# Scanning two tiles at a time, small products on VectorE, and a prologue in another order

## The chip, the cores and the metric

The kernel runs on one core of a Trainium2 chip. The metric is device time in microseconds (us) of one execution. "The span" is the time between the first and the last instruction that the profile shows; the device time of the same execution is a little longer.

## The reference

Three parts follow each other. A linear recurrence (a "state space" scan, here ssm) over 4 batches x 8 heads x 768 positions turns x into y. A dense layer with a gate follows, and then a mixture of eight experts with one expert per token. The core of it:

```python
L = np.exp(cum[:, :, :, None] - cum[:, :, None, :]) * causal
M = np.einsum('bhin,bhjn->bhij', Cc, Bc) * L
y_intra = np.einsum('bhij,bhjd->bhid', M, xc)
y_inter = np.einsum('bhin,bhnd->bhid', Cc, state) * np.exp(cum)[:, :, :, None]
y[:, :, sl] = y_intra + y_inter
state = decay_full[:, :, None, None] * state + np.sum(Bx, axis=2)
...
h = x @ w_in
x = (h * (1.0 / (1.0 + np.exp(-1.702 * h)))) @ w_out
...
expert_idx = np.argmax(logits, axis=1)
out[mask] = gate_w[mask, None] * (np.maximum(x[mask] @ w1[e], 0.0) @ w2[e])
```

There are 3072 tokens, 256 features, 2048 hidden columns in the dense layer, and 8 experts with 1024 hidden columns.

## The kernel before

**Tiles and groups.** The 3072 tokens are 24 tiles of 128 positions; three tiles are a group, so there are groups 0 to 7. A tile holds two chunks of 64 positions, and six tiles are one batch, at whose start the state is empty. The dense layer cuts its 2048 hidden columns into 16 slices f. A **block** (g, f) is `gemm1` (six matmuls of 384 columns, `ph`), `gate` (two ScalarE activations), `low_part` (one VectorE subtraction, `glb`) and `gemm2` (nine matmuls of 256 columns into `po`). Every product runs as three matmuls, on high parts and low parts of both operands, hence yh and yl, and two tiles of each weight (`dw0`, `dw1`).

**The scan of a tile.** `A` scales x (`xtb`). `U` is `ssm_c` (matmuls `pU`) and `ssm_b` (matmuls `pS`). `T` is `ssm_state` (the recurrence on VectorE, `T`), `ssm_pads` (`S`, the state masked for two heads, on GpSimd) and `ssm_mask` (`mt`, on VectorE). `Y` is `ssm_d` (matmuls `pY`, which read mt, xtb and S). `E` is `ssm_e` (`ye` = pY times `ee`, VectorE), `ssm_h` (yh, a cast on ScalarE) and `ssm_l` (yl, a subtraction on GpSimd). pS and pY share one PSUM buffer. `ee` is an exponential per position; for group 0 it is computed on the core (`edge`, `edge_exp`), for the others all rows are computed once (`edge_scale`, matmuls into `ph` and an activation `et`), written to DRAM (`ebuf`) and read back broadcast (`load_ee`).

**The order.** Every engine executes in the order in which the code emits. The string `START` is the prologue, one letter and a number for each step: X and x are edge and edge_exp, N and W load a tile's or a slice's data, A U S T s M Y E H L are the scan's parts, R B u p v h l decode the 16 weight slices from 64-bit words into high and low parts, G g c O are gemm1, gate, low_part and gemm2 of the n-th block, F fills slots in DRAM, r are parts of the router (r4 is edge_scale), i is load_ee, z a route0. The prologue runs the 32 blocks of groups 0 and 1, in turns, and the scans of tiles 0 to 8. A "'" behind a step moves it to its other engine.

After it come six passes `pi` = 1 to 6 of 16 blocks each, for group 2, 3, ..., 7. Within pass pi the tiles of group pi+2 are scanned, each in four steps at a block offset: U and T at k, Y at k+2, E at k+3, with k = 2, 6, 10 (2, 6, 11 in pass 1). The router of the group before (route0 to route4) runs in the same pass. Two blocks are always pending between gemm1 and gemm2, so the last two gemm2 of a group run in the next pass, route0 then copies po (three copies: tile 2 and 0 on VectorE, tile 1 on ScalarE), and the next group's first gemm2 writes the same PSUM. The experts follow behind the passes.

All DMAs but the scatters are issued from SP's queue, in the order of the code, and a DMA whose data or buffer isn't ready holds what is behind it.

Of the kernel before, what the change touches and what calls it, by code (L numbers as in the profile page):

```python
# [10 lines left out]
F32 = mybir.dt.float32  # L11
# [124 lines left out]
def body(ctx, tc, ssm, aall, cst, tok, wcat, emb, tau, w1, w2, out):  # L136
# [39 lines left out]
    sp = early.enter_context(tc.tile_pool(name="sp", bufs=2))  # L176
    late = ExitStack()
# [22 lines left out]
    def load_ee(g):  # L200
        ee = sp.tile([P, TPG, 2, P], F32, tag="ee", name=f"ee{g}")
# [51 lines left out]
    def edge(g):  # L253

        pee = psy.tile([P, 2, 512], F32, tag="sy", name=f"pee{g}")
        cols = al[:, :NTILE * NH].rearrange("p (g q t) -> p g q t", g=NG, q=4)[:, g]
        for j in range(2 * TPG):
            w, o = divmod(j * P, TPG * P)
            for q in range(4):
                nc.tensor.matmul(pee[32 * q:32 * q + 32, w, o:o + P], lhsT=cols[:, q, j:j + 1].to_broadcast([P, 32]),  # L260
                                 rhs=tri, start=(o == 0), stop=True, skip_group_check=True)
        ee_s[g] = pee

    def edge_exp(g):
        pee = ee_s[g]
        ee = sp.tile([P, TPG, 2, P], F32, tag="ee", name=f"ee{g}")
        nc.scalar.activation(out=ee.rearrange("p t k c -> p (t k c)").rearrange("p (w c) -> p w c", w=2),
                             in_=pee[:, :, :TPG * P], func=AF.Exp)
        ee_s[g] = ee
# [55 lines left out]
    def decode_mask(f):  # L325
        v = sp.tile([P, 512], F32, tag="v", name=f"v{f}")
# [14 lines left out]
    Ts = {}  # L341

    def ssm_a(t, eng=nc.gpsimd):
        b, tt = divmod(t, TPB)
        xt = xtb[t % NXT]
        e0 = (b * NCH + 2 * tt) * NPAIR
        eng.tensor_tensor(
            out=xt.rearrange("p c q d -> p (c q) d"), in0=raw_s[t][:, SB2 + SBT:SB2 + SBT + SX].rearrange("p (c d) -> p c d", d=HD),
            in1=einv[:, e0:e0 + 2 * NPAIR].unsqueeze(2).to_broadcast([P, 2 * NPAIR, HD]), op=ALU.mult)
        st.setdefault(t, {})["xt"] = xt  # L350

    def ssm_b(t):

        r = raw_s[t]
        ps = (pre if t < NPRE else psy).tile([P, 2, 512], F32, tag="sy", name=f"pS{t}")
        for c in range(2):
            for w in range(2):
                h = slice(64 * w, 64 * w + 64)
                nc.tensor.matmul(ps[:, w, c * P:(c + 1) * P].rearrange("p (k i) -> p k i", k=2),  # L359
                                 lhsT=r[h, c * P:(c + 1) * P], rhs=cpad(t)[h, :, c, :],  # L360
                                 start=(c == 0), stop=True, skip_group_check=True)
        st.setdefault(t, {})["ps"] = ps

    def ssm_mask(t):
        ps = st[t]["ps"]
        mt = sp.tile([P, 2, 2, 2, Q], F32, tag="mt", name=f"mt{t}")
        nc.vector.tensor_tensor(out=mt.rearrange("p w c k i -> p w (c k) i"),
                                in0=ps[:, :, :256].rearrange("p w (c i) -> p w c i", i=Q),
                                in1=kc[:, K_MASK:K_MASK + Q].unsqueeze(1).unsqueeze(1).to_broadcast([P, 2, 4, Q]),
                                op=ALU.mult)  # L370
        st[t]["mt"] = mt

    def ssm_c(t):
        r, xt = raw_s[t], st[t]["xt"]
        pu = pss.tile([P, 512], F32, tag="m", name=f"pU{t}")
        for c in range(2):
# [4 lines left out]
        st[t]["pu"] = pu  # L381

    def ssm_state(t):

        b, tt = divmod(t, TPB)
        pu = st[t]["pu"]
        e0 = b * NCH + 2 * tt
# [19 lines left out]
    def ssm_pads(t, eng=nc.gpsimd):

        b, tt = divmod(t, TPB)
        c0 = 1 if tt == 0 else 0  # L410
        e0 = b * NCH + 2 * tt + c0 - 1
        n = 2 - c0
        S = sp.tile([P, 2, 2, HD], F32, tag="S", name=f"S{t}")
        eng.tensor_tensor(out=S[:, c0:], in0=Ts[t][:, c0:, :].unsqueeze(2).to_broadcast([P, n, 2, HD]),
                          in1=decm[:, e0:e0 + n, :].unsqueeze(3).to_broadcast([P, n, 2, HD]), op=ALU.mult)
        st[t]["sps"] = [None if c < c0 else S[:, c] for c in range(2)]
        del Ts[t]

    def ssm_d(t):
        xt, mt, sps = st[t]["xt"], st[t]["mt"], st[t]["sps"]  # L420
        py = psy.tile([P, 2, 512], F32, tag="sy", name=f"pY{t}")
# [6 lines left out]
        for c in range(2):  # L428
# [11 lines left out]
        st[t]["py"] = py  # L440

    def ssm_e(t):
        g, tl = divmod(t, TPG)
        py = st[t]["py"]
        if tl == 0:
            yh[g] = yp.tile([P, 2, GT], F32R, tag="yh", name=f"yh{g}")
            yl[g] = yp.tile([P, 2, GT], F32R, tag="yl", name=f"yl{g}")
        ye = sp.tile([P, 2, P], F32, tag="ye", name=f"ye{t}")
        nc.vector.tensor_tensor(out=ye, in0=py[:, :, :P], in1=ee_s[g][:, tl], op=ALU.mult)
        st[t]["ye"] = ye  # L450

    def ssm_h(t, eng=None):
        g, o = t // TPG, t % TPG * P
        (eng.tensor_copy if eng else nc.scalar.copy)(out=yh[g][:, :, o:o + P], in_=st[t]["ye"])  # L454

    def ssm_l(t, eng=nc.gpsimd):
        g, o = t // TPG, t % TPG * P
        ye = st[t]["ye"]
        eng.tensor_tensor(out=yl[g][:, :, o:o + P], in0=ye, in1=yh[g][:, :, o:o + P].bitcast(F32), op=ALU.subtract)  # L459
        del st[t], raw_s[t]  # L460
# [721 lines left out]
```

## Time and profile before

| | |
|---|---|
| three runs | 543.3, 544.15, 544.98 us (median 544.15) |
| the profiled execution | 543.77 us, its span 542.0 us |
| TensorE (PE) busy | 511.6 us of the span |
| VectorE (DVE), ScalarE (ACT), GpSimd (POOL) busy | 335.4, 245.9, 135.0 us |
| one block on PE, nothing between | 2.11 us (1.05 gemm1, 1.06 gemm2) |
| pass 2, from one first gemm2 to the next | 160.30 to 201.08 us |

PE is the engine to watch: where it has no pause, only fewer or cheaper instructions on it help; where it pauses, the question is what it waits for. In a timeline each row is a start, a duration, an engine, a line of the code, an operation, its tiles and a count; a bracket at its end is the time that the engine sat idle before it and what ended that. fp32 matmuls of the scan show two records for each instruction.

### The profile page before, as it was taken

What the parts mean: (1) busy time and instruction counts of PE and PEld (TensorE: products, weight loads), DVE (VectorE), ACT (ScalarE), POOL (GpSimd) and SP (SyncE); (2) the same over time, 40 slices, a digit from 0 to 9 for tenths busy, and PEclk for the clock granted to TensorE, in tenths of its full rate; (3) what the DMA queues carried; (4) which work ended last, traced back from release to release, by engine and by line L of the source; (5) the groups of instructions that cost most, each with busy time, mean ns of one, the idle gap of its engine ahead of it and who ended that gap; (6) DMA issues with size and microseconds to landing.
All of it is one profiled execution on the core that took longest, in us unless ns stands there. A gap on an engine that the chain in (4) does not pass through costs nothing.

```text
span 542.0 us, 13468 instructions
## 1 busy us (share of the span) xinstructions
PE 511.6 (94%) x5392; PEld 485.6 (90%) x5392; DVE 335.4 (62%) x969; ACT 245.9 (45%) x573; POOL 135.0 (25%) x168
## 2 busy tenths in 40 slices
PE   5779999999999999999999999999999999999991
PEld 4569999889989999999999999989999999999991
DVE  3658777766757667657667655866767666555330
ACT  4638666334344344344344344852645435444220
POOL 3433443201431042042042020412311030232022
PEclk9979999989999999999999999999999999999996
DMA  8886874211221121120000005370466442511000
GB/s 304 232 261 183 310 198 143 80 70 40 69 100 40 41 99 40 42 98 2 1 30 2 2 32 195 108 234 20 166 211 207 128 149 96 161 40 49 10 28 28
DMA packets 29052, 57.59 MB, mean 106 GB/s; under 512 B 2790, under 2 KB 19004, under 8 KB 28860
## 3 DMA queue, kind: packets, MB, share of 16 engines
q1 hardware_dynamic: 26492, 50.39, 28.8%
q0 software_dynamic: 2496, 6.32, 3.1%
q8 instruction: 43, 0.70, 0.5%
q14 instruction: 21, 0.17, 0.1%
HBM read 46.05 MB, written 11.01 MB: 105 GB/s over the span
## 4 chain that ended last, share of the span: by engine, by line
PE 70%; issue 13%; DMA 6%; POOL 3%; ACT 2%; DVE 2%; SPq 0%; POOLq 0%; ACTq 0%; DVEq 0%
PE ph L516 21%; PE po L541 17%; PE ph L741 9%; PE qo L767 9%; PE po_a L541 5%; PE pS L359 2%; DMA ee<-ebuf 2%; POOL out L141 2%; DMA wraw<-in_wcat 2%; PE pY L431 2%; PE pY L438 1%; PE pU L379 1%; PE pX L727 1%; DMA slots<-xr,si 1%; DMA wer<-in_w 1%
## 5 line engine op out<-in xcount | busy, mean ns | idle before, releaser
L516 PE MATMUL ph<-yh,dw 128*128 128x384 f32 x512 | 157.2, 347 | 2.5 <-DVE yh L454 1.5
L525 ACT ACTIVATE ghb<-ph 128x384 fp32r<-128x384 f32 x128 | 62.8, 490 | 124.7 <-PE ph L516 124.4
L533 DVE TENSOR_TENSOR glb<-ph,ghb 128x384 fp32r<-128x384 f32 x128 | 70.9, 554 | 74.6 <-ACT ph L526 74.4
L541 PE MATMUL po<-dw,ghb 128*128 128x256 f32 x576 | 107.2, 282 | 1.6 <-ACT xr L554 1.6
L516 PEld LDWEIGHTS ph<-yh,dw 128*128 128x128 f32 x512 | 95.1, 189 | 7.5 <-DVE yh L454 1.6
L541 PEld LDWEIGHTS po<-dw,ghb 128*128 128x128 f32 x576 | 93.1, 188 | 3.3 <-ACT xr L554 3.3
L516 PE MATMUL ph<-yl,dw 128*128 128x384 f32 x256 | 86.6, 338 | 0.5 <-POOL yl L459 0.4
L541 PE MATMUL po<-dw,glb 128*128 128x256 f32 x288 | 81.0, 281 | 0.0
L748 DVE SCALAR_TENSOR_TENSOR glb<-ph,ghb 128x256 fp32r<-128x256 f32 (+5 forms) x72 | 36.6, 508 | 46.3 <-ACT ghb L747 46.1
L747 ACT ACTIVATE ghb<-ph 128x256 fp32r<-128x256 f32 (+5 forms) x72 | 32.6, 453 | 65.7 <-PE ph L741 65.7
L526 ACT ACTIVATE ph<-ph 128x384 f32<-128x384 f32 x128 | 62.2, 486 | 0.0
L141 POOL DMA_INDIRECT out<-ob,xs x29 | 29.8, 1029 | 123.3 <-DVE ob L778 117.3
L767 PE MATMUL qo<-weh,ghb 128*128 128x256 f32 x208 | 58.7, 282 | 0.0
L767 PE MATMUL qo<-wel,ghb 128*128 128x256 f32 x208 | 58.5, 281 | 0.0
L767 PE MATMUL qo<-weh,glb 128*128 128x256 f32 x208 | 58.5, 281 | 0.0
L541 PEld LDWEIGHTS po<-dw,glb 128*128 128x128 f32 x288 | 54.5, 189 | 0.0
L741 PE MATMUL ph<-xh,weh 128*128 128x256 f32 (+5 forms) x160 | 52.7, 329 | 0.6 <-ACT xh L728 0.2
L741 PE MATMUL ph<-xl,weh 128*128 128x256 f32 (+5 forms) x160 | 51.5, 322 | 0.5 <-DVE xl L729 0.4
L741 PE MATMUL ph<-xh,wel 128*128 128x256 f32 (+5 forms) x160 | 51.2, 320 | 0.0
L516 PEld LDWEIGHTS ph<-yl,dw 128*128 128x128 f32 x256 | 48.6, 190 | 1.1 <-POOL yl L459 0.6
L595 DVE SCALAR_TENSOR_TENSOR pr<-xr,enb 128x256 f32<-128x256 f32 x120 | 48.0, 434 | 0.5
L693 DVE TENSOR_TENSOR wel<-wer,weh 128x512 fp32r<-128x512 f32 x60 | 44.7, 749 | 4.4 <-ACT weh L692 3.4
(188 smaller groups left out, 884.7 us busy)
## 6 DMA issues: line engine op xcount, KB each, us to landing
wer<-in_w SPq DMA_DIRECT2D x32, 512.0 KB, 4.1
raw<-in_ssm SPq DMA_DIRECT2D x24, 512.0 KB, 5.3
wraw<-in_wcat SPq DMA_DIRECT2D x16, 512.0 KB, 9.8
slots<-padr SPq DMA_DIRECT2D x8, 516.0 KB, 7.2
ee<-ebuf SPq DMA_DIRECT2D x7, 384.0 KB
xs<-slots SPq DMA_DIRECT2D x3, 516.0 KB, 4.1
xs<-slots SPq DMA_DIRECT2D x3, 387.0 KB
xs<-slots SPq DMA_DIRECT2D x4, 258.0 KB
```

Source lines behind the costliest of these rows:

```text
L141: i = nc.gpsimd.indirect_dma_start(in_offset=None, oob_is_err=False, **kw)
L516: nc.tensor.matmul(ph, lhsT=wslice(w, f, k * P, k * P + P), rhs=y[g][:, k, :], start=(n == 0), stop=(n == 5))
L525: nc.scalar.activation(out=a[:, :GT], in_=ph, func=AF.Gelu_apprx_sigmoid)
L526: nc.scalar.activation(out=ph, in_=ph, func=AF.Gelu_apprx_sigmoid)
L533: nc.vector.tensor_tensor(out=c[:, :GT], in0=ph, in1=a[:, :GT].bitcast(F32), op=ALU.subtract)
L541: nc.tensor.matmul(po[g][tl], lhsT=l, rhs=r, start=(f == 0 and i == 0 and (off + tl) % 2 == 0), stop=(f == NF - 1 and i == 2), skip_group_ ...
L595: nc.vector.scalar_tensor_tensor(out=pr, in0=xr[:, tl, :D], scalar=1.0, in1=enb[:, e, :], op0=ALU.mult, op1=ALU.mult, accum_out=ld[:, tl, ...
L693: eng.tensor_tensor(out=lo[:, o], in0=r, in1=hi[:, o].bitcast(F32), op=ALU.subtract)
L741: nc.tensor.matmul(ph[:, :n], lhsT=w[:, o:o + P], rhs=x[u][:, k, :n], start=(i == 0), stop=(i == 5))
L747: nc.scalar.activation(out=a[:, :n], in_=ph[:, :n], func=AF.Relu)
L748: nc.vector.scalar_tensor_tensor(out=c[:, :n], in0=ph[:, :n], scalar=0.0, in1=a[:, :n].bitcast(F32), op0=ALU.max, op1=ALU.subtract)
L767: nc.tensor.matmul(qacc(u, s), lhsT=l, rhs=r, start=(f == 0 and i == 0 and (s % 2 == 0 or ss is not None)), stop=(f == NFE - 1 and i == 2) ...
```

## The change

It does five things.

1. `START` is written anew. Group 1's ee is computed on the core (X1, x1) and no longer read back (i1 is gone); edge_scale (r4) stands earlier; the fills F stand later; tile 6, 7 and 8 stand apart, over some ten blocks, where they stood close to the end.
2. From tile 10 on, the scan takes a **unit**: a pair (t, 2), or the single tile 9. `ahead` lists the units of each pass. The matmuls are as many as before; the VectorE and ScalarE instructions on a pair take twice the columns, but for `ssm_state`, which stays at one for each chunk.
3. In the passes `ssm_pads` and `ssm_l` run on VectorE.
4. `gemm2` of the first slice of groups 2 to 7 takes its three tiles from the last to the first.
5. Decode buffers have a pool of their own, which is closed before the passes and leaves room for the pairs; ee has three buffers.

```diff
 START = (
-    "X0 W0 x0 u0 N0 N1 S0 B0 W1 A0' U0 N2 W2 M0 S1 R0 T0 N3 p0 R1 A1 u1 U1 T1 s0' Y0 r4 M1 A2 E0 p1 U2 T2 s1 v0 "
+    "W0 u0 B0 X0 x0 R0 N0 S0 A0 M0 U0 N1 W1 B1 N2 R1 N3 T0 s0 p0 v0 r4 W2 u1 N4 h0 S1 A1 U1 T1 M1 A2 Y0 E0 U2 T2 "
...
     def edge(g):
 
-        pee = psy.tile([P, 2, 512], F32, tag="sy", name=f"pee{g}")
+        if g == 0:
+            pee = psy.tile([P, 2, 512], F32, tag="sy", name="pee0")
+            pee = [pee[:, w, :] for w in range(2)]
+        else:
+            pee = [hbank() for _ in range(2)]
...
+    def ssm_c(u):
+        t0, n = unit(u)
+        xt = st[t0]["xt"]
+        pu = pss.tile([P, 512], F32, tag="m", name=f"pU{t0}")
+        for c in range(2 * n):
+            r = raw_s[t0 + c // 2]
             for p in range(NPAIR):
-                o = SB2 + (c * NPAIR + p) * 32
+                o = SB2 + (c % 2 * NPAIR + p) * 32
                 nc.tensor.matmul(pu[32 * p:32 * p + 32, c * HD:(c + 1) * HD], lhsT=r[:, o:o + 32],
                                  rhs=xt[:, c, p, :], start=True, stop=True)
...
     def step(t, what):
         for fn in {"A": (ssm_a,), "U": (ssm_c, ssm_b), "T": (ssm_state, ssm_pads, ssm_mask), "Y": (ssm_d,),
                    "E": (ssm_e, ssm_h, ssm_l)}[what]:
-            fn(t)
+            if fn in (ssm_pads, ssm_l):
+                fn(t, nc.vector)
+            else:
+                fn(t)
...
-        for tl in range(TPG):
+        for tl in (range(TPG) if f or g < 2 else reversed(range(TPG))):
...
-    def tile_steps(jobs, t0, at):
-        for i, k in enumerate(at):
+    def unit_steps(jobs, us, at):
+        for u, k in zip(us, at):
             for d, w in ((0, "U"), (0, "T"), (2, "Y"), (3, "E")):
-                jobs.append((k + d, lambda t=t0 + i, w=w: step(t, w)))
...
+    ahead = {1: [9, (10, 2)], 2: [(12, 2), (14, 2)], 3: [(16, 2)], 4: [(18, 2), (20, 2)], 5: [(22, 2)]}
...
-        if gn < NG:
-            tile_steps(jobs, TPG * gn, (2, 6, 11) if pi == 1 else (2, 6, 10))
...
+        if pi in ahead:
+            unit_steps(jobs, ahead[pi], (3, 10) if pi == 1 else (2, 8))
```

**TensorE in the prologue.** The rows from group 0's ee on (pee0); the number behind a tile's name is the tile of 128 positions, the one behind "_" is a buffer's. ph_287 and ph_247 are edge_scale. Before:

```order
L260 MATMUL pee0_167<-kc_102,al_103 32x128 x24
L359 MATMUL pS0_203<-raw0_199 128x128 x4
L379 MATMUL pU0_213<-xtb0_109,raw0_199 32x32 x8
L359 MATMUL pS1_228<-raw1_201 128x128 x4
L379 MATMUL pU1_248<-xtb1_110,raw1_201 32x32 x8
L431 MATMUL pY0_262<-mt0_226,xtb0_109 32x64 x16
L438 MATMUL pY0_262<-raw0_199,S0_260 32x64 x8
L275 MATMUL ph_287<-kc_102,al_103 96x128 x2
```

With the change (ph_376 and ph_377 are group 1's ee):

```order
L266 MATMUL pee0_177<-kc_105,al_106 32x128 x24
L374 MATMUL pS0_209<-raw0_207 128x128 x4
L398 MATMUL pU0_217<-xtb0_112,raw0_207 32x32 x8
L282 MATMUL ph_247<-kc_105,al_106 96x128 x2
L374 MATMUL pS1_261<-raw1_226 128x128 x4
L398 MATMUL pU1_267<-xtb1_113,raw1_226 32x32 x8
L450 MATMUL pY0_282<-mt0_215,xtb0_112 32x64 x16
L457 MATMUL pY0_282<-raw0_207,S0_242 32x64 x8
L398 MATMUL pU2_311<-xtb2_114,raw2_232 32x32 x8
L374 MATMUL pS2_327<-raw2_232 128x128 x4
L266 MATMUL ph_376<-kc_105,al_106 32x128 x12
L266 MATMUL ph_377<-kc_105,al_106 32x128 x12
```

edge_scale moved from behind tile 0's pY to behind tile 0's pU, and 24 matmuls for group 1's ee are new; between pS2 and them stand tile 1's two pY rows, not shown here.

**SP's queue at the start.** wraw is a slice of weights (W), raw a tile's data (N). Before:

```order
L219 DMA wraw2_224<-in_wcat 128x512
L209 DMA raw3_239<-in_ssm 128x1024
L278 DMA ebuf_82<-et_290 96x2x128
L219 DMA wraw3_422<-in_wcat 128x512
L209 DMA raw4_427<-in_ssm 128x1024
L219 DMA wraw6_459<-in_wcat 128x512
L203 DMA ee1_503<-ebuf_82 128x1x768
```

With the change:

```order
L211 DMA raw3_236<-in_ssm 128x1024
L285 DMA ebuf_82<-et_250 96x2x128
L221 DMA wraw2_253<-in_wcat 128x512
L211 DMA raw4_258<-in_ssm 128x1024
L221 DMA wraw3_454<-in_wcat 128x512
L221 DMA wraw6_473<-in_wcat 128x512
L211 DMA raw5_525<-in_ssm 128x1024
```

The third slice of weights (wraw2) now stands behind the write of ebuf, and the load of ee1 is gone.

**TensorE in pass 2,** where tile 12 is scanned; po2 is a gemm2 of group 2, ph a gemm1 of group 3. Before:

```order
L541 MATMUL po2_1_2338<-dw1_0_151,ghb1_90 128x256
L541 MATMUL po2_1_2338<-dw0_0_147,glb1_94 128x256
L379 MATMUL pU12_2367<-xtb0_109,raw12_1932 32x32 x8
L359 MATMUL pS12_2376<-raw12_1932 128x128 x4
L516 MATMUL ph_2389<-yh3_1838,dw0_0_147 128x384
```

With the change:

```order
L582 MATMUL po2_0_2369<-dw0_0_150,glb1_94 128x256
L398 MATMUL pU12_2399<-xt12_2217,raw12_1925 32x32 x8
L398 MATMUL pU12_2399<-xt12_2217,raw13_1994 32x32 x8
L374 MATMUL pS12_2416<-raw12_1925 128x128 x4
L374 MATMUL pS12_2416<-raw13_1994 128x128 x4
L557 MATMUL ph_2435<-yh3_1920,dw0_0_150 128x384
```

Tile 13's matmuls, which stood four blocks later between two other blocks, now follow tile 12's of the same kind.

## Rows read from the trace of the kernel before

**Rows 1.** The page: span, and busy time of the engines.

```profile
span 542.0 us, 13468 instructions
PE 511.6 (94%) x5392; PEld 485.6 (90%) x5392; DVE 335.4 (62%) x969; ACT 245.9 (45%) x573; POOL 135.0 (25%) x168
```

**Rows 2.** Timeline of PE, the prologue's start.

```profile
5.98 2.77 PE L260 MATMUL pee<-kc,al 128*32 128x128 f32 x48
...
30.49 1.22 PE L359 MATMUL pS<-raw 64*128 64x128 f32 x8 [5.33 <-DVE ye L449]
...
41.08 0.44 PE L516 MATMUL ph<-yh,dw 128*128 128x384 f32 x1
```

**Rows 3.** Timeline of DVE, the prologue's start.

```profile
10.69 0.69 DVE L367 TENSOR_TENSOR mt<-pS,kc 128x512 f32<-128x512 f32 x1 [0.87 <-PE pS L359]
...
23.83 0.53 DVE L404 SCALAR_TENSOR_TENSOR T<-T,dec,pU 128x32 f32<-128x32 f32 x2
30.01 0.42 DVE L449 TENSOR_TENSOR ye<-pY,ee 128x256 f32<-128x256 f32 x1 [5.66 <-DMA ee<-ebuf]
```

**Rows 4.** Timeline of SP's queue, the prologue's start.

```profile
15.88 0.34 SPq L278 DMA_DIRECT2D ebuf<-et  x1
```

**Rows 5.** Stretches: us, busy time by engine, PE's granted clock, DMA share, GB/s.

```profile
32.00:34.00 2.00, 2.00 (x20) 1.77 (x22) 1.33 (x2) 1.51 (x3) 1.75 (x3) 0.50 0.95 343
...
40.00:60.00 20.00, 19.95 (x152) 19.08 (x151) 17.44 (x36) 15.48 (x32) 7.42 (x5) 1.00 0.77 238
```

**Rows 6.** The page: DMA issues, KB each, median us to landing.

```profile
raw<-in_ssm SPq DMA_DIRECT2D x24, 512.0 KB, 5.3
wraw<-in_wcat SPq DMA_DIRECT2D x16, 512.0 KB, 9.8
```

**Rows 7.** Timeline of PE, later in the prologue and in pass 1.

```profile
67.99 0.62 PE L516 MATMUL ph<-yh,dw 128*128 128x384 f32 x2 [0.69 <-POOL dw L335]
...
82.67 0.34 PE L516 MATMUL ph<-yh,dw 128*128 128x384 f32 x1
...
84.78 0.34 PE L516 MATMUL ph<-yh,dw 128*128 128x384 f32 x1
...
109.24 0.44 PE L516 MATMUL ph<-yh,dw 128*128 128x384 f32 x1 [1.49 <-DVE yh L454]
...
115.44 0.34 PE L516 MATMUL ph<-yh,dw 128*128 128x384 f32 x1
```

**Rows 8.** Timeline of PE, end of pass 1.

```profile
154.59 0.44 PE L516 MATMUL ph<-yl,dw 128*128 128x384 f32 x1 [0.36 <-POOL yl L459]
```

**Rows 9.** Timeline of PE in pass 2.

```profile
164.68 0.34 PE L516 MATMUL ph<-yh,dw 128*128 128x384 f32 x1
...
169.75 0.34 PE L516 MATMUL ph<-yh,dw 128*128 128x384 f32 x1
...
171.95 0.33 PE L379 MATMUL pU<-xtb,raw 128*32 128x32 f32 x16
172.22 0.71 PE L359 MATMUL pS<-raw 64*128 64x128 f32 x8
172.86 0.44 PE L516 MATMUL ph<-yh,dw 128*128 128x384 f32 x1
...
175.08 0.34 PE L516 MATMUL ph<-yh,dw 128*128 128x384 f32 x1
...
180.28 0.34 PE L516 MATMUL ph<-yh,dw 128*128 128x384 f32 x1
```

**Rows 10.** Groups by line and shape: busy us, mean ns, idle before and releaser.

```profile
L541 PE MATMUL po<-dw,ghb 128*128 128x256 f32 x576 | 107.2, 282 | 1.6 <-ACT xr L554 1.6
...
L533 DVE TENSOR_TENSOR glb<-ph,ghb 128x384 fp32r<-128x384 f32 x128 | 70.9, 554 | 74.6 <-ACT ph L526 74.4
...
L367 DVE TENSOR_TENSOR mt<-pS,kc 128x512 f32<-128x512 f32 x24 | 16.5, 687 | 2.8 <-PE pS L359 2.2
...
L404 DVE SCALAR_TENSOR_TENSOR T<-T,dec,pU 128x32 f32<-128x32 f32 x40 | 9.8, 244 | 4.0 <-PE pU L379 3.2
```

More of the change, by code (lines that the diff above doesn't have):

```diff
@@ L265, in edge_exp @@
         pee = ee_s[g]
-        ee = sp.tile([P, TPG, 2, P], F32, tag="ee", name=f"ee{g}")
-        nc.scalar.activation(out=ee.rearrange("p t k c -> p (t k c)").rearrange("p (w c) -> p w c", w=2),
-                             in_=pee[:, :, :TPG * P], func=AF.Exp)
+        ee = sp.tile([P, TPG, 2, P], F32, tag="ee", name=f"ee{g}", bufs=3)
+        for w in range(2):
+            nc.scalar.activation(out=ee.rearrange("p t k c -> p (t k c)")[:, w * TPG * P:(w + 1) * TPG * P],
+                                 in_=pee[w][:, :TPG * P], func=AF.Exp)
         ee_s[g] = ee
@@ L341, in body, with unit, ssm_a, ssm_b @@
     Ts = {}
[L343 to L356, printed above, removed]
+    pairs = {}
+    def unit(u):
+        return u if isinstance(u, tuple) else (u, 1)
+    def ssm_a(u, eng=nc.gpsimd):
+        t0, n = unit(u)
+        xt = pairs["p"].tile([P, 4, NPAIR, HD], F32, tag="xt", name=f"xt{t0}") if "p" in pairs else xtb[t0 % NXT]
+        for t in range(t0, t0 + n):
+            o = 2 * (t - t0)
+            e0 = 2 * t * NPAIR
+            eng.tensor_tensor(
+                out=xt[:, o:o + 2].rearrange("p c q d -> p (c q) d"),
+                in0=raw_s[t][:, SB2 + SBT:SB2 + SBT + SX].rearrange("p (c d) -> p c d", d=HD),
+                in1=einv[:, e0:e0 + 2 * NPAIR].unsqueeze(2).to_broadcast([P, 2 * NPAIR, HD]), op=ALU.mult)
+        st.setdefault(t0, {})["xt"] = xt
+    def ssm_b(u):
+        t0, n = unit(u)
+        ps = (pre if t0 < NPRE else psy).tile([P, 2, 512], F32, tag="sy", name=f"pS{t0}")
+        for c in range(2 * n):
+            r = raw_s[t0 + c // 2]
             for w in range(2):
@@ L373, in ssm_c, with ssm_mask @@
[L373 to L376, printed above, removed]
+        st.setdefault(t0, {})["ps"] = ps
+    def ssm_mask(u):
+        t0, n = unit(u)
+        ps = st[t0]["ps"]
+        mt = (pairs["p"].tile([P, 2, 4, 2, Q], F32, tag="mt", name=f"mt{t0}") if "p" in pairs else
+              sp.tile([P, 2, 2, 2, Q], F32, tag="mt", name=f"mt{t0}"))
+        nc.vector.tensor_tensor(out=mt[:, :, :2 * n].rearrange("p w c k i -> p w (c k) i"),
+                                in0=ps[:, :, :256 * n].rearrange("p w (c i) -> p w c i", i=Q),
+                                in1=kc[:, K_MASK:K_MASK + Q].unsqueeze(1).unsqueeze(1).to_broadcast([P, 2, 4 * n, Q]),
+                                op=ALU.mult)
+        st[t0]["mt"] = mt
@@ L383, in ssm_state @@
[L383 to L387, printed above, removed]
+        st[t0]["pu"] = pu
+    def ssm_state(u):
+        t0, n = unit(u)
+        pu = st[t0]["pu"]
         def slot(nt):
             if nt not in Ts:
-                Ts[nt] = sp.tile([P, 2, HD], F32, tag="T", name=f"T{nt}", bufs=3)
+                Ts[nt] = sp.tile([P, 4, HD], F32, tag="T", name=f"T{nt}", bufs=3)
             return Ts[nt]
-        for c in range(2):
-            ch = 2 * tt + c
+        for c in range(2 * n):
+            i = 2 * t0 + c
+            ch = i % NCH
@@ L405, in ssm_state @@
                                                op1=ALU.add)
[L407 to L417, printed above, removed]
@@ L419, in ssm_d, with ssm_pads @@
-    def ssm_d(t):
-        xt, mt, sps = st[t]["xt"], st[t]["mt"], st[t]["sps"]
-        py = psy.tile([P, 2, 512], F32, tag="sy", name=f"pY{t}")
+    def ssm_pads(u, eng=nc.gpsimd):
+        t0, n = unit(u)
+        c0 = 1 if 2 * t0 % NCH == 0 else 0
+        e0 = 2 * t0 + c0 - 1
+        m = 2 * n - c0
+        S = sp.tile([P, 4, 2, HD], F32, tag="S", name=f"S{t0}")
+        eng.tensor_tensor(out=S[:, c0:2 * n], in0=Ts[t0][:, c0:2 * n, :].unsqueeze(2).to_broadcast([P, m, 2, HD]),
+                          in1=decm[:, e0:e0 + m, :].unsqueeze(3).to_broadcast([P, m, 2, HD]), op=ALU.mult)
+        st[t0]["sps"] = [None if c < c0 else S[:, c] for c in range(2 * n)]
+        del Ts[t0]
@@ L427, in ssm_d @@
         heads = [(k, q, r) for q in range(2) for k in range(2) for r in range(2)]
-        for c in range(2):
+        for c in range(2 * n):
             for k, q, r in heads:
@@ L432, in ssm_d @@
                                  start=(c == 0), stop=True, skip_group_check=True)
-        for c in range(2):
+        for c in range(2 * n):
             if sps[c] is None:
@@ L437, in ssm_d @@
                 h = slice(32 * (2 * k + q), 32 * (2 * k + q) + 32)
-                nc.tensor.matmul(place(k, q, r, c), lhsT=sps[c][h, r, :], rhs=cpad(t)[h, q, c, :],
+                nc.tensor.matmul(place(k, q, r, c), lhsT=sps[c][h, r, :], rhs=cpad(t0 + c // 2)[h, q, c % 2, :],
                                  start=False, stop=True, skip_group_check=True)
[L440 to L460, printed above, removed]
+        st[t0]["py"] = py
+    def parts(u):
+        t0, n = unit(u)
+        if n == 1 or (t0 + 1) % TPG:
+            return [(t0, n)]
+        return [(t0, 1), (t0 + 1, 1)]
@@ new lines, in ssm_e @@
+    def ssm_e(u):
+        t0, n = unit(u)
+        py = st[t0]["py"]
+        ye = (pairs["p"] if n == 2 else sp).tile([P, 2, n * P], F32, tag=f"ye{n}", name=f"ye{t0}")
+        for t, m in parts(u):
+            g, tl = divmod(t, TPG)
+            if tl == 0:
+                yh[g] = yp.tile([P, 2, GT], F32R, tag="yh", name=f"yh{g}")
+                yl[g] = yp.tile([P, 2, GT], F32R, tag="yl", name=f"yl{g}")
+            o = slice((t - t0) * P, (t - t0 + m) * P)
+            ee = ee_s[g][:, tl:tl + m].rearrange("p t k c -> p k t c")
+            nc.vector.tensor_tensor(out=ye[:, :, o].rearrange("p k (t c) -> p k t c", c=P),
+                                    in0=py[:, :, o].rearrange("p k (t c) -> p k t c", c=P), in1=ee, op=ALU.mult)
+        st[t0]["ye"] = ye
@@ new lines, in ssm_h, with ssm_l @@
+    def ssm_h(u, eng=None):
+        for t, m in parts(u):
+            g, o, i = t // TPG, t % TPG * P, (t - unit(u)[0]) * P
+            (eng.tensor_copy if eng else nc.scalar.copy)(out=yh[g][:, :, o:o + m * P],
+                                                         in_=st[unit(u)[0]]["ye"][:, :, i:i + m * P])
+    def ssm_l(u, eng=nc.gpsimd):
+        t0, n = unit(u)
+        ye = st[t0]["ye"]
+        for t, m in parts(u):
+            g, o, i = t // TPG, t % TPG * P, (t - t0) * P
+            eng.tensor_tensor(out=yl[g][:, :, o:o + m * P], in0=ye[:, :, i:i + m * P],
+                              in1=yh[g][:, :, o:o + m * P].bitcast(F32), op=ALU.subtract)
+        del st[t0]
+        for t in range(t0, t0 + n):
+            del raw_s[t]
@@ L1001, in body @@
                 jobs += [(12, lambda: route2(gp)), (14, lambda: route3(gp)), (15, lambda: route4(gp))]
-        if gn < NG:
-            tile_steps(jobs, TPG * gn, (2, 6, 11) if pi == 1 else (2, 6, 10))
-        if gn + 1 < NG:
-            tile_loads(jobs, TPG * (gn + 1), 7)
-            jobs += [(13, lambda t=TPG * (gn + 1) + i: step(t, "A")) for i in range(TPG)]
-            jobs.append((14, lambda: load_ee(gn + 1)))
+        if pi == 1:
+            dp_ctx.close()
+            pairs["p"] = early.enter_context(tc.tile_pool(name="pp", bufs=2))
+            jobs += [(0, lambda u=u: step(u, "A")) for u in ahead[1]]
+        if pi in ahead:
+            unit_steps(jobs, ahead[pi], (3, 10) if pi == 1 else (2, 8))
+        nxt = ahead.get(pi + 1, [])
+        for i, t in enumerate(t for u in nxt for t in range(unit(u)[0], sum(unit(u)))):
+            jobs.append((6 + 2 * i, lambda t=t: load_ssm(t)))
+        jobs += [(12 + 2 * i, lambda u=u: step(u, "A")) for i, u in enumerate(nxt)]
+        for g in sorted({t // TPG for u in nxt for t, _ in parts(u)}):
+            if g not in loaded:
+                loaded.add(g)
+                jobs.append((14, lambda g=g: load_ee(g)))
         if pi + 1 == len(passes):
```

50 lines of the change are left out of this document (24 added, 26 removed), and 24 rows, old and new, of the table START.

## The prediction

> **What bounds the kernel now.** I read the page first: PE is busy for 511.6 of 542.0 us, DVE for 335.4, POOL for 135.0 [rows 1]. So the change can gain in two ways only: by pauses of PE that end earlier, and by scan matmuls that take less of PE's time. Work that moves between DVE and POOL counts only where PE waits for it.
>
> I then went through PE's timeline for pauses. The largest after the first data is 5.33 us, ended by a VectorE `ye` [rows 2]. DVE's timeline says why: it was at work from 10.69 to 24.36 us, then stood 5.66 us in front of the ye of tile 3, which needed group 1's ee out of DRAM [rows 3]. That ee was late because the write of ebuf, which it reads, was issued only at 15.88 us [rows 4]. [...]
>
> Later pauses in the prologue are 0.69 us for a decoded weight and 1.49 us at 109.24, where gemm1 of group 2 waits for the yh of tile 8 [rows 7]. From 109.24 to 115.44 lie two blocks, 6.20 us, while one block takes 84.78 - 82.67 = 2.11 us [rows 7]. In the passes PE has almost no pause: 0.36 us for yl [rows 8] and 1.6 us in all for the copy xr [rows 10].
>
> What the scan costs PE in a pass comes from the starts of gemm1 around it [rows 9]. From 169.75 to 175.08 are two blocks with one U step: 5.33 - 4.22 = 1.11 us. From 175.08 to 180.28 are two blocks with one Y step of 64 matmul records: 5.20 - 4.22 = 0.98 us. From 164.68 to 169.75 are two blocks with the Y of a batch's first tile, 48 records: 0.85 us.
>
> **The change, part by part.** *Start of the prologue, -5.3 us.* PE no longer sets the pace there; DVE does, and it works in the order of the code. Before the ye of tile 3 it executes, from the first mt on, 27 instructions before and 28 after. After has in addition a half-width S, two yl and a v; it lacks an S, a lo part and a yl. At 0.42 us for a yl (ye of the same shape [rows 3]) and, for v and lo, the 0.69 of an mt of their width [rows 3], that is +0.3 us, an S counted at 0.42. So that ye can start at 24.4 + 0.3 = 24.7 in place of 30.01: 5.3 us earlier, if no new wait stands in DVE's queue. From there to group 1's first gemm1, 11.1 us before [rows 2, 3], the same work follows, in a slightly other order; I count it as equally long.
>
> Two things may use this up. The 48 records of group 1's ee take at most the 2.77 us of group 0's [rows 2]; PE has room for them while it waits for DVE, so I count nothing, and 2.8 as the bound. The third slice of weights is now issued behind ebuf. Its decode stands in DVE's queue ahead of tile 3's ye, with 4 us of work between. ebuf itself moves ahead by a U, an S and a Y, to some 13.5 us by the rows' durations, and not beyond 15.88. A load lands 5.3 us (raw) or 9.8 us (wraw) after its issue in the median [rows 6]: at 18.8 us at best, harmless, or at 25.7, which takes the whole gain. I take the first, since only one raw is queued ahead of it there, while most wraw stand behind others. Bounds of this term: 0 and 7.5 us, the latter if the clock doesn't fall either and PE does its part of the 11.1 us faster.
>
> *End of the prologue, -3.5 us.* Tile 8's last steps now stand some eight blocks ahead of group 2's gemm1, in place of directly ahead. The 1.49 us go, and so does what the lower clock added behind it, 6.20 - 4.22 = 2.0 us. What hides tile 8's chain are those eight blocks, 17 us; without them the 1.49 return. Bounds 1.5 and 4.2 (with the 0.69 for the weight, which I don't count, since the weights are wanted 5 us earlier now).
>
> *Pairs, -4.3 us.* Tiles 9 to 23 take 15 U and 15 Y steps before, 8 and 8 after: 7 of each go, while the number of matmuls stays. What one saves is what a step costs apart from its records. For Y: 16 records more cost 0.98 - 0.85 = 0.13 us; at that rate 64 cost 0.52, and 0.46 is left for the step. For U: 16 pU at the same rate are 0.13, the 8 pS take 172.86 - 172.22 = 0.64, and 0.34 is left. 7 x 0.80 = 5.6 us is the upper bound. The lower is nothing, if the costs go with the records after all. I take 4.3, nearer the upper, because the split of U rests on one row, and because the one pair of rows that differs only in the number of records speaks for a fixed part. [...] A pair's DVE work is no new wait: four T at 0.244, S at about 0.42, and an mt of 1024 columns at 0.69 + 2 x 0.27 = 1.23 us (0.27 is what 256 columns more cost between ye and mt [rows 3, 10]) end some 3 us after pU, and Y comes two blocks, 4.2 us, after U. Behind them on DVE stand the router's products and the next glb (0.55 us [rows 10]), which PE needs only behind Y.
>
> *gemm2 from the last tile to the first, -1.6 us.* Route0 frees tile 2's PSUM first. Starting there, PE finds the other two freed 0.36 us later (three matmuls). The 1.6 us of waits for xr go; bounds 0 and 1.9.
>
> *yl and S on VectorE, -0.4 us.* The one wait of a gemm1 for POOL's yl goes [rows 8]; elsewhere POOL's lateness was hidden. DVE has the room: 17.4 of 20 us busy is its highest stretch, and that is in the prologue [rows 5]. Later fills, the A steps and the ee loads are hidden behind whole blocks.
>
> The sum is 5.3 + 3.5 + 4.3 + 1.6 + 0.4 = 15.1 us. The profiled execution took 543.77 us, so 528.7. It lies 0.4 us under the median of the three runs, 544.15, which is less than they differ.
>
> **The rivals.** *The lead is lost to the weights.* The third slice lands late, or PE arrives 5 us earlier at slices whose decode is not faster. For it speaks the 0.69 us wait, which ended on a lo part of a weight, and DVE at 87% and ACT at 77% from 40 to 60 us [rows 5]. Against it: the fills, eight loads of 0.5 MB, now stand behind most weights. The 5.3 us are lost: 534.0.
>
> *Pairs bring nothing*, because each record pays its own price, or because DVE's longer chain makes PE wait what the pair saved. Against it stands the 0.13 us row. 528.7 + 4.3 = 533.0.
>
> *More than counted*: the clock stays up through the start, and the pairs save all that is fixed: 2.2 + 1.3 + 0.7 (the weight) more, 524.5.
>
> *Slower: decoding becomes the bound.* Each slice of weights feeds two blocks, 4.2 us of PE. 17.44 us of DVE in 20 [rows 5] are 3.7 us for each such 4.2; the new order gives it one yl or S more here and there and puts hi and lo parts on queues that other steps share. If every slice from the fourth to the sixteenth were late by more than 15.1 / 13 = 1.2 us, so that DVE's round took 5.4 us in place of 3.7, the gain would be gone: 543.8 or more. I see no row that adds so much.
>
> **How the numbers follow.** The forecast 0.50, the lead lost 0.18, pairs without effect 0.12, more than counted 0.13, decoding as the bound 0.07. A measurement of this kernel tells about 0.3%, 1.6 us, from no change; only the last case falls inside or beyond that, so faster 0.93, same 0.03, slower 0.04. The upper bounds together are 7.5 + 4.2 + 5.6 + 1.9 + 0.4 = 19.6, which gives 524.2; if a quarter of pS's 0.64 us also goes with each step, 7 x 0.16 = 1.1 more do, and the range begins at 523. It ends at 536, the lead lost and half of the pairs' gain with it.
>
> **What would show it.** Right: tile 3's ye starts near 25 us with no wait for a DMA; the first gemm1 of group 1 near 35; no pause at the first gemm1 of group 2 and no lower clock there, about 7 us ahead of 109.24; two blocks with a pair's U between them take some 1.9 us more than 4.2, not 2.2; no wait of a gemm2 for xr. Wrong: a wait of DVE for wraw before 30 us, waits of gemm1 for weights between 35 and 100 us, or a pause of PE in front of a pair's pY.

## The result, and the profile after

| | before | after |
|---|---|---|
| median of 4 runs | 544.08 us (543.3 to 544.98) | 531.66 us (530.03 to 532.37) |
| ratio | | 0.9767, 95% interval 0.9739 to 0.9795 |
| the profiled execution, its span | 543.77, 542.0 us | 532.37, 530.6 us |

Faster by 12.4 us; the forecast of 528.7 lies 15.4 us under the same median of before. A second series of the same kernel gave 0.9766 (0.974 to 0.9792). The time is inside the range; one term of the sum is not what the prediction made of it.

The page of the kernel after, its span and the busy time of the engines (answers to [rows 1]):

```profile
span 530.6 us, 13540 instructions
PE 505.3 (95%) x5440; PEld 485.9 (92%) x5440; DVE 338.8 (64%) x970; ACT 245.6 (46%) x570; POOL 120.9 (23%) x144
```

TensorE has 48 records more (group 1's ee) and is still busy for 6.3 us less. By stretches: 1.4 us more up to group 1's first gemm1 at equal work (26.55 before, 27.94 after; equal work is explained below), 2.5 less from there to group 2's first gemm2 (74.84 and 72.37), and 5.2 less between there and the end of the dense layer (238.79 and 233.59), where steps of the scan are merged. Its timeline at the start (answers to [rows 2]):

```profile
14.96 0.33 PE L398 MATMUL pU<-xtb,raw 128*32 128x32 f32 x16 [1.69 <-DVE T L422]
...
16.79 1.52 PE L266 MATMUL ph<-kc,al 128*32 128x128 f32 x48
18.24 0.46 PE L450 MATMUL pY<-mt,xtb 64*32 64x64 f32 x32
18.62 0.42 PE L457 MATMUL pY<-raw,S 32*32 32x64 f32 x22
22.07 0.44 PE L457 MATMUL pY<-raw,S 32*32 32x64 f32 x10 [3.03 <-issue]
...
39.17 0.34 PE L557 MATMUL ph<-yh,dw 128*128 128x384 f32 x1
```

The 5.33 us that ended on tile 3's ye are gone. A new pause of 3.03 us stands in the middle of tile 2's pY: 22 of 32 records have run, the other 10 wait, and the profile names no tile and no engine for it, only "issue". VectorE's timeline (answers to [rows 3]):

```profile
19.43 0.69 DVE L325 SCALAR_TENSOR_TENSOR u<-wraw,u 128x512 int32<-128x512 int32 x1
22.58 0.42 DVE L479 TENSOR_TENSOR ye<-pY,ee 128x256 f32<-128x256 f32 x1 [2.45 <-PE pY L457]
...
26.54 0.42 DVE L479 TENSOR_TENSOR ye<-pY,ee 128x256 f32<-128x256 f32 x1 [0.27 <-PE pY L457]
```

VectorE waits for tile 2's pY, hence for that pause, and tile 3's ye (26.54) waits for no DMA, as said, but is 1.8 us later than the 24.7 of the sum. Two stretches of the same execution, with the columns of [rows 5]:

```profile
14.00:20.00 6.00, 4.01 (x190) 3.17 (x191) 5.90 (x15) 2.01 (x4) 3.10 (x4) 1.00 0.91 321
20.00:34.00 14.00, 10.91 (x219) 8.54 (x218) 8.30 (x19) 7.99 (x16) 6.97 (x9) 0.53 0.53 207
```

From 20 to 34 us the granted clock is 0.53 in the mean, and 0.50 from 21 us on. Before, it was as low from 28 to about 35 us (0.51 from 28 to 30, 0.56 from 34 to 35, 1.00 on either side).

The end of the prologue and pass 2, on PE:

```profile
106.19 0.34 PE L557 MATMUL ph<-yh,dw 128*128 128x384 f32 x1
...
111.69 0.48 PE L582 MATMUL po<-dw,ghb 128*128 128x256 f32 x2
...
169.07 0.35 PE L557 MATMUL ph<-yh,dw 128*128 128x384 f32 x1
...
171.30 0.46 PE L398 MATMUL pU<-xt,raw 128*32 128x32 f32 x32
171.69 1.16 PE L374 MATMUL pS<-raw 64*128 64x128 f32 x16
172.78 0.44 PE L557 MATMUL ph<-yh,dw 128*128 128x384 f32 x1
...
175.00 0.34 PE L557 MATMUL ph<-yh,dw 128*128 128x384 f32 x1
...
177.20 0.86 PE L450 MATMUL pY<-mt,xt 64*32 64x64 f32 x64
177.99 0.85 PE L457 MATMUL pY<-raw,S 32*32 32x64 f32 x64
178.78 0.44 PE L557 MATMUL ph<-yh,dw 128*128 128x384 f32 x1
...
181.01 0.34 PE L557 MATMUL ph<-yh,dw 128*128 128x384 f32 x1
```

Group 2's first gemm1 (106.19) has no bracket: the 1.49 us are gone, and the granted clock is 1.00 from 104 to 111.69 (before, it was 0.72 in the mean from 109.24 to 115.44). But it stands 3.05 us ahead of the 109.24 of before, where about 7 were foretold. From 169.07 to 175.00 lie two blocks and a pair's U: 5.93 - 4.22 = 1.71 us, where two single U take 2.22. From 175.00 to 181.01 lie two blocks and a pair's Y of 128 records: 1.79, where two single Y take 1.96. The waits of PE from 45 us on (us in total, times, longest):

```profile
PE pX L768 <- DMA xs<-slots: 0.8, 1, 0.8
PE ph L557 <- DVE glb L574: 0.3, 1, 0.3
PE ph L782 <- ACT xh L769: 0.2, 1, 0.2
```

No gemm2 waits for xr, and no gemm1 for weights or yl.

**Where the 11.4 us of span come from.** The first gemm2 of group 2 starts at 116.55 before and 111.69 after: 4.9. From there to the last two gemm2 of the dense layer, which run in one go from 358.51 and 346.45 on, before takes 241.96 and after 234.76: 7.2. From there to the end, 183.5 and 184.1: -0.6. To cut the prologue in two, the first gemm1 of group 1 won't do as it stands: before had run a third gemm2 (from 39.17) and tile 6's pS (from 40.44) ahead of the 41.08 of [rows 2], after has not. That gemm2 takes 1.07 us in after (38.10 to 39.17), the pS 0.64, 1.71 in all; with the same work done, before stands at 39.37 and after at 39.17. (The two rows of before take 1.91 us, since the first two records of that gemm2 take 0.51 us there and 0.40 in after, and its row 1.27 in all; by them before would stand at 39.17 too.) So the start gave 0.2 us at most in this execution, and the rest of the prologue 4.7.

### The profile page after: what moved, and what is told of

Its sections match the earlier page's. It is cut to its first block, busy times and chain, and to the rows that moved or that the text cites. A ratio compares the mean times of both kernels' runs of the same rounds, so it can differ in the third digit from the quotient of the medians.

```text
span 530.6 us, 13540 instructions
## 1 busy us (share of the span) xinstructions
PE 505.3 (95%) x5440; PEld 485.9 (92%) x5440; DVE 338.8 (64%) x970; ACT 245.6 (46%) x570; POOL 120.9 (23%) x144
## 4 chain that ended last, share of the span: by engine, by line
PE 78%; issue 12%; DVE 2%; POOL 2%; DMA 2%; ACT 1%; POOLq 0%; ACTq 0%; SPq 0%
PE ph L557 25%; PE po L582 18%; PE ph L782 9%; PE qo L808 9%; PE po_a L582 7%; PE pS L374 3%; POOL out L141 2%; PE pY L450 2%; PE pY L457 2%; PE pX L768 1%; DMA slots<-xr,si 1%; PE pU L398 1%; PE pL L654 1%; DMA xs<-slots 1%; DMA al<-in_aall 1%
## 5 line engine op out<-in xcount | busy, mean ns | idle before, releaser
L141 POOL DMA_INDIRECT slots<-xr,si x24 | 24.5, 1021 | 155.9 <-DVE xr L705 117.0
```

The lines of the kernel that those rows point to most:

```text
L141: i = nc.gpsimd.indirect_dma_start(in_offset=None, oob_is_err=False, **kw)
```

## The experiments

Each is the changed kernel with one edit. The code shown is an excerpt, with "..." where lines are left out. "First gemm2" is group 2's first one in the profiled execution (before 116.55, after 111.69), and "the stretch" runs from there to the last two gemm2 of the dense layer (after 234.76 us).

**forward**: no reversed tile order in gemm2.

```diff
-        for tl in (range(TPG) if f or g < 2 else reversed(range(TPG))):
+        for tl in range(TPG):
...
```

> The changed kernel with gemm2 of the first slice in the old tile order. If the 1.6 us of waits for xr return as they stood in the trace of before: 533.3 us, and the trace shows five waits of gemm2 for xr of about 0.3 us each. If the router's copies end early enough without them in the passes of pairs: 531.7 us, no such wait.

533.53 us, ratio 0.979 (0.9761 to 0.982). The interval overlaps that of the changed kernel, so the time alone tells nothing; the list of PE's waits does:

```profile
PE po L582 <- ACT xr L595: 1.6, 5, 0.3
```

The five waits are back, and the stretch is 236.88 us, 2.1 more. The term stands.

**singles**: one tile at a time in the passes.

```diff
-    ahead = {1: [9, (10, 2)], 2: [(12, 2), (14, 2)], 3: [(16, 2)], 4: [(18, 2), (20, 2)], 5: [(22, 2)]}
+    ahead = {p: [3 * p + 6 + i for i in range(3)] for p in range(1, 6)}
...
-            unit_steps(jobs, ahead[pi], (3, 10) if pi == 1 else (2, 8))
+            unit_steps(jobs, ahead[pi], (2, 6, 11) if pi == 1 else (2, 6, 10))
```

> The changed kernel with the tiles 9 to 23 scanned one by one in the passes, U and T at blocks 2, 6, 10 as before. Theory, from the trace of the changed kernel: a pair's U costs two blocks 1.71 us and a pair's Y 1.80 (1.66 at a batch's start), singles 1.11 and 0.98 (0.85), so seven pairs save 7 x (0.51 + 0.16) = 4.7 us: 536.4 us. Rival, pairs save nothing on the whole because what the fixed part saves returns elsewhere: 531.7 us.

535.24 us, ratio 0.9834 (0.9801 to 0.9866), 3.6 us over the changed kernel; in the trace the stretch is 239.30 us, 4.5 more. The pairs do save PE time; the rival falls.

**small_on_pool**: S and yl of the passes on GpSimd.

```diff
-                fn(t, nc.vector)
+                fn(t, nc.gpsimd)
```

> The changed kernel with S and yl of the passes on GpSimd again. Theory: only the one wait for yl comes back, 0.4 us, below what a measurement can tell: 531.7 to 532.1 us. Rival, with pairs the small products are twice as wide, and GpSimd ends a pair's S or yl too late for Y or for the next group's gemm1: 533 us or more, with waits of PE for S or yl in the trace.

531.29 us, ratio 0.9757 (0.9728 to 0.9785): the same. PE waits for no S and no yl, and the stretch is 234.47 us. The 0.4 us were not to be had there; GpSimd is in time for pairs too.

**old_start**: the prologue's string of before, without A9, A10, A11.

> The changed kernel with the prologue string of before (its A steps of tiles 9 to 11 left out, since the passes do them). By the prediction's terms the new order is worth 5.3 + 3.5 = 8.8 us: 540.5 us. By the traces, the first gemm2 of group 2 at 116.50 before and 111.69 after, it is worth 4.8 us: 536.5 us.

537.48 us, ratio 0.9863 (0.9829 to 0.9897), first gemm2 at 115.95. The new order is worth about 5.2 us by the ratios: nearer the traces' 4.8 than the prediction's 8.8. The two ratios come from different series, and by their intervals the 5.2 is uncertain by some 2 us. The wait for ee<-ebuf is there again (4.82 us on VectorE in front of tile 3's ye).

**hold**: a DMA of 512 bytes that needs tile 1's ye, on SP's queue in front of five loads.

```diff
+    hold_d = drp.tile([1, P], F32, name="holdd")
+    def hold(t):
+        nc.sync.dma_start(out=hold_d, in_=st[t]["ye"][:1, 0, :P])
...
-    "... B2 L0' E1 X1 A3 l0' H1 L1' Y2 R2 U3 u2 p2 W3 ..."
+    "... B2 L0' E1 q1 X1 A3 l0' H1 L1' Y2 R2 U3 u2 p2 W3 ..."
```

> The changed kernel with one more small DMA on SP's queue that needs tile 1's ye (about 18 us), ahead of the loads of slices 3, 6, 4, 5 and tile 5, which so start some 4 us later; nothing else moves. Theory: TensorE's pause of 3.0 us in the pY of tile 2, which the trace puts to no tile, is its next instructions, whose 16 KB stand behind these loads in the DMA engines; without the loads the pause falls below 0.6 us, the clock falls later or not at all, and the time is 528 to 530 us. Rival: the instructions are asked for too late whatever the DMA engines do; the pause stays at 1.7 us or more and the time at 531.7 us.

530.36 us, ratio 0.9775 (0.9738 to 0.9811). The held loads start at 18.43 us in place of 14.58. The pause is gone from tile 2's pY. SP's queue, PE's timeline, and the columns of [rows 5] from 20 us on, in the variant:

```profile
18.08 0.30 SPq L982 DMA_DIRECT2D holdd<-ye  x1
18.43 0.83 SPq L209 DMA_DIRECT2D wraw<-in_wcat  x2
```

```profile
16.78 2.79 PE L254 MATMUL ph<-kc,al 128*32 128x128 f32 x48
19.50 0.66 PE L438 MATMUL pY<-mt,xtb 64*32 64x64 f32 x32
20.09 0.47 PE L445 MATMUL pY<-raw,S 32*32 32x64 f32 x32
...
26.08 0.27 PE L362 MATMUL pS<-raw 64*128 64x128 f32 x1 [0.43 <-issue]
...
34.43 0.34 PE L545 MATMUL ph<-yh,dw 128*128 128x384 f32 x1
```

```profile
20.00:34.00 14.00, 12.13 (x345) 9.41 (x330) 11.30 (x26) 8.90 (x19) 8.45 (x10) 1.00 0.72 264
```

All 32 records of tile 2's pY run in one go, the clock, 0.58 in the mean from 16 to 20 us, is 1.00 from 20 to 34, tile 3's ye starts at 23.88, and the first gemm1 of group 1 stands at 34.43 in place of 39.17. What had been late shows in the DMA view, queue by queue with packets, MB and share of the 16 engines. In the kernel after, the 0.1 us from 19.6:

```profile
q1 hardware_dynamic: 13, 0.05, 110.4%
q8 instruction: 1, 0.02, 54.9%
```

A packet of the kind "instruction" (0.02 MB) lies among the data there, from 19.65 on; PE went on at 22.07, 2.4 us later. In this variant the packet is found between 17.0 and 17.5, ahead of need, where the engines are busy for 0.52 of the time with data:

```profile
q1 hardware_dynamic: 33, 0.11, 52.5%
q8 instruction: 1, 0.02, 15.3%
```

The pause part of the expectation holds, with one reserve. PE comes to the record of the pause at 20.27 here and at 19.04 in after, since group 1's ee, at the low clock, took 2.79 us in place of 1.52. A packet that starts at 17.07 lets PE go on at about 19.5, if the 2.4 us hold here too; so some 0.4 us of the 3.03 are gone by PE's lateness, and the rest by the packet. The time does not follow: the first gemm2 comes 4.5 us earlier (107.22), the median is no lower than can be told from the changed kernel's. In the profiled execution 2.3 us of the lead are lost behind it, most where the experts begin: besides the wait for rows out of DRAM that after has too, PE waits 0.67 and 0.40 us for their casts and 0.7 for a glb.

**ee_loaded**: group 1's ee read back directly behind ebuf, X1 and x1 gone.

```diff
-    "... p0 v0 r4 W2 u1 N4 ..."
+    "... p0 v0 r4 i1 W2 u1 N4 ..."
```

> The changed kernel with group 1's ee read back from DRAM, as before, but directly behind the write of ebuf, in place of 48 matmul records on the core. Theory: the read lands by 20 us, ahead of tile 3's ye, TensorE has 1.5 to 2.8 us less to do where it is also short of instructions, and the time is 529 to 531 us: the ee needn't be computed on the core. Rival: it lands behind slice 2 and later than 25 us, VectorE waits for it again in front of tile 3's ye, and the time is 534 us or more.

536.72 us, ratio 0.9876 (0.9847 to 0.9904). The rival's time, but by another wait: not the ee is late, the slice behind it is. PE, VectorE and ScalarE:

```profile
28.50 1.22 PE L362 MATMUL pS<-raw 64*128 64x128 f32 x8 [8.73 <-DVE ye L467]
```

```profile
26.62 0.43 DVE L482 TENSOR_TENSOR yl<-ye,yh 128x256 fp32r<-128x256 f32 x1 [7.97 <-ACT yh L474]
```

```profile
25.63 0.66 ACT L305 ACTIVATE ab<-wraw 128x512 f32<-128x512 f32 x1 [9.63 <-DMA wraw<-in_wcat]
```

ScalarE stood 9.63 us in front of slice 2, with tile 1's yh queued behind that, VectorE behind the yh for 8.0 us, and PE behind VectorE. Tile 3's ye then waited for no DMA. This is the prediction's risk to the first term, at a larger size. Whether the read would do behind slice 2 was not tried.

**scan_first**: v of slice 0 and u of slice 1 behind the first tiles' T, mt and ye on VectorE; h of slice 0 and p and v of slice 1 move along with them.

```diff
-    "... p0 v0 r4 W2 u1 N4 h0 S1 A1 U1 T1 M1 A2 Y0 E0 U2 T2 H0 p1 v1 S2 M2 s1' Y1 s2' B2 L0' E1 X1 ..."
+    "... p0 r4 W2 N4 S1 A1 U1 T1 M1 A2 Y0 E0 U2 T2 H0 v0 h0 S2 M2 u1 s1' Y1 s2' p1 B2 L0' E1 v1 X1 ..."
```

> The changed kernel with the steps v of slice 0 and u of slice 1 behind the T, mt and ye of the first tiles on VectorE. They stand ahead of tile 1's T and make TensorE wait 1.7 us in front of pU of tile 2. Theory, with the instructions as the bound: that wait goes, TensorE runs out of instructions earlier and waits there as much longer: 531 to 532 us. Rival, VectorE sets the pace: 530 us.

531.04 us, ratio 0.9775 (0.9746 to 0.9804). The wait for T is gone, and PE has won nothing by it:

```profile
21.95 0.32 PE L445 MATMUL pY<-raw,S 32*32 32x64 f32 x10 [3.28 <-issue]
```

It is at the same record of the same pY, waits 3.28 us, and goes on within 0.12 us of the 22.07 of the kernel after. VectorE does not set the pace here; PE goes on 2.5 us behind an instruction packet (19.46). (The median can't tell the two apart: its interval overlaps that of the changed kernel.)

**hold_scan_first**: both.

> Both edits together, the held loads and the scan's steps first. Theory, both pauses go, 1.7 + 3.0 us, and the clock stays up: 526 to 528 us. Rival, instructions asked for too late: 531 us.

531.27 us, ratio 0.9784 (0.9753 to 0.9814). The packet comes between 17.5 and 18.0, but PE is at the record earlier still:

```profile
20.16 0.32 PE L445 MATMUL pY<-raw,S 32*32 32x64 f32 x10 [1.74 <-issue]
```

With fewer loads in flight the pause is half as long, and not gone. The theory fell: the time is the rival's. So the rival of **hold** is right in part: without the hold the packet comes later (19.46 in scan_first, 17.83 here), and a TensorE that is at the record sooner (18.42 here, 20.27 in **hold**) waits all the same.

**after_again**: no edit.

> The changed kernel once more. Its first profiled execution had the granted clock at 0.5 for some 13 us from 20.6 us on, three variants with the same prologue for some 5 us. Theory, that stretch differs from execution to execution: the first gemm2 of group 2 at 109 to 110 us this time in place of 111.69, median 531 to 532 us. Rival, the long stretch belongs to this kernel: 111.7 us again.

532.25 us, ratio 0.9766 (0.974 to 0.9792). First gemm2 at 112.17, the clock 0.56 in the mean from 20 to 34 us: in the one trace the long stretch came back, as the rival said. But the granted clock over the whole of each execution speaks for the theory. Of the five executions two have 0.977 and 0.976, at 532.61 (the profiled one) and 533.13 us, and three have 0.983 to 0.985, at 530.31 to 532.25. Of **small_on_pool**'s six three have 0.977 to 0.980, at 532.31 to 532.40, and three have 0.983 to 0.987, at 529.12 to 530.27; the profiled one, with the short stretch, has 0.987. So executions of one kernel differ, and one trace doesn't tell how the others went.

**hold_pool**: **hold** and **small_on_pool** together.

> The held loads together with S and yl of the passes on GpSimd, the two variants that stood lowest. Theory, the 2 us by which the held loads bring group 2's first gemm2 forward reach the end: 529 to 530 us. Rival, what is gained before 110 us is lost again where the experts wait for rows and weights out of DRAM: 531 us.

529.45 us, ratio 0.9731 (0.9709 to 0.9754), in the same series as after_again. This is the lowest median of the study, 2.8 us under it and where the theory had it, though the two intervals still overlap by 0.0014, so that its lead is not shown. First gemm2 at 108.71; a pause of 0.73 us is left in tile 2's pY and one of 0.87 in a pS.

**start_only**: single tiles, GpSimd and the old tile order in the passes; only the prologue is new.

> The changed kernel with single tiles, S and yl on GpSimd and the old tile order of gemm2 in the passes, so that only the prologue (with its pools) is new. Theory, the parts add up: the prologue alone is worth 4.8 us by the profiled execution and 6 to 7 by the others of the same prologue, 537 to 539 us. Rival, the prologue's lead is lost in the passes of singles: 541 us or more.

538.42 us, ratio 0.9886 (0.986 to 0.9912): the prologue alone is worth 5.5 us against the before of its series. First gemm2 at 112.01. The step from here to after_again, same series, is 6.2 us for the passes, where 6.3 were forecast. The two steps add up to the whole by construction; what they add is that the prologue is worth about the same with the old passes (5.5) as with the new ones (5.2 by **old_start**).

## Why the prediction was right, and where not

The time lies in the range, and partly by luck: none of the prediction's signs of being wrong came, and yet its largest term failed; the end of the prologue and the passes gave back 2.1 of the 5.1 us that it missed, and the part behind the dense layer took 0.6 us more than before.

- **Start of the prologue, -5.3 forecast, 0.2 in the profiled execution.** This term failed, by its condition "if no new wait stands in DVE's queue". The late ee was rightly named and is gone, slice 2 was not late (VectorE's u on it ran at 18.99), and no weight held a gemm1. What came is a wait that the prediction had not among its rivals: from 19.04 on TensorE stood 3.03 us on "issue", and went on 2.4 us behind an instruction packet. The step that failed is "The 48 records of group 1's ee ... PE has room for them ... so I count nothing": they and the earlier tiles bring PE 3.5 us sooner to the same place in its program (346 records done at 22.54 before, where it waited 0.28 us for "issue"; 348 at 19.04 after), but PE went on only 0.75 us sooner, at 22.07 in place of 22.82.

  That the 48 records by themselves bring the pause is not shown: **ee_loaded**, which lacks them, met another wait first. The long stretch at the lower clock behind the pause (0.53 in the mean from 20 to 34 us) took the rest. In **forward**, **singles** and **small_on_pool**, with the same prologue, the pause and a shorter such stretch, the first gemm1 of group 1 stands at 36.66 to 37.46, 1.9 to 2.7 us ahead of the 39.37 at equal work; in after_again and start_only it stands at 39.70 and 39.51, behind it. With the loads held back it stood at 34.43, 4.9 us ahead, in the one trace without the pause: that is near what the term would have been. "Near 35" itself was a slip: by the sum, 24.7 + 11.1, it was due at 35.8, and that counted the third gemm2 and tile 6's pS (1.7 us) as ahead of that gemm1, where they stand behind it now. The bound of 7.5 has 2.2 us more for a clock that doesn't fall. That a pause of PE brings the fall no run shows by itself: behind the same wait of 1.69 us in front of a pU the clock is 1.00 up to 20 us in after (PE goes on at 14.96) and 0.58 in the mean from 16 to 20 us in **hold** (PE goes on at 14.89).
- **End of the prologue, -3.5: 4.7.** No pause, no lower clock, as said; the 0.69 us for a weight, which stood in the bound only, went too; with them the bound was 4.2, and 0.5 is not told apart.
- **Pairs, -4.3: 4.5 by singles' trace, 3.6 by its ratio.** The size is right, the split behind it is not. A pair's U saves 0.51 us, more than the 0.34 taken as fixed; a pair's Y only 0.17, not 0.46. The step that failed is the rate of 0.13 us for 16 records: the 64 records more of a pair's Y cost 1.79 - 0.98 = 0.81, or 0.20 for 16. The upper bound, 5.6 with the whole fixed part gone at each step, the Y rows do not bear out.
- **gemm2 reversed, -1.6: 1.6 in waits** (2.1 in the stretch). Right.
- **yl and S on VectorE, -0.4: nothing**; the wait stays away with GpSimd too, as long as tiles are paired. With single tiles on GpSimd (**start_only**) it is there, 0.4 us.

So 6.3 of the passes came as forecast (6.2 by start_only), and the prologue gave 4.9 to 5.5 of 8.8. The rival "lead is lost to the weights" foresaw a lost start for another reason and gave 534.0; the time came out between it and the forecast, because the end of the prologue gave 1.2 us more and the stretch 0.9 more than forecast.

What stays open: in three profiled executions with this prologue (after, after_again, start_only) the mean granted clock from 20 to 34 us is 0.53 to 0.56, in three others (forward, singles, small_on_pool) 0.76 to 0.88, with first gemm2 at 109.2 to 109.9 in place of 111.7 to 112.2. The pause on "issue", 1.66 to 3.54 us, is in all six. By the clocks of whole executions (**after_again**) this differs between executions of one kernel; what decides was not found, so a difference of 2 us between two single traces proves nothing about an edit. And why **hold**, with the start in order, doesn't show its lead in the median was seen in one trace only.

## What to carry to other kernels

Where TensorE runs many small matmuls while loads fill the DMA engines (0.91 of their time from 14 to 20 us here), look for pauses that end on "issue" in the middle of a group, and for packets of the kind "instruction" ahead of them; in **scan_first**, where the wait for an operand (1.69 us) was gone, the pause there was 3.28 us in place of 3.03. Holding back loads that aren't needed yet shortened that pause or ended it in the three variants that did so (1.74 and 0.73 us left, and none); that it also pays in time was not shown here. Two steps merged into one saved the part of a step that does not go with its records (0.51 us for a U, 0.17 for a Y), and one row with a few records more was too little to tell that part: take the rate from rows that differ by as many records as the merge does. Compare two orders at equal work, not at the first instruction of one name.

## What the runs showed of the hardware

Instructions are part of the DMA traffic: the page of the kernel after has 43 packets with 0.70 MB on queue q8, kind "instruction", 16 KB each in the mean. That they are TensorE's no view says; the times speak for it. The pause comes behind the same 22 of 32 records of tile 2's pY (348 records of PE in after) in the traces of after, after_again, start_only, scan_first, hold_scan_first and hold_pool, and PE goes on 2.3 to 2.5 us behind the start of a packet, wherever that lies: 17.83 and on at 20.16 (hold_scan_first), 18.14 and 20.64 (hold_pool), 19.46 and 21.95 (scan_first), 19.65 and 22.07 (after), 20.03 and 22.41 (after_again), 20.38 and 22.68 (start_only), 20.42 and 22.82 (before, behind 346 records). With the loads held the packet starts at 17.07 to 18.14 us (three executions), without that, in the new prologue, at 19.46 to 20.38 (the other four). So in these traces the time of the packet goes with the loads, and PE's going on with the packet; whether the packet queues behind the loads or is asked for later is not shown. Beside those 43 packets, PE's list of waits in after has one pause on "issue", this one of 3.03 us; in after_again, scan_first and start_only it is 2.64, 3.28 and 3.54 us.
